# Joined VectorE products and a permuted fine-factor read in an S4 convolution on one Trainium2 core

## The chip, the core and the metric

The kernel runs on one core of a Trainium2 chip. Five engines work side by side there, each with its own instruction stream: TensorE (PE in the profile, with its weight loads as PEld), VectorE (DVE), ScalarE (ACT), GpSimd (POOL) and SyncE (SP). The last two serve here mostly to issue DMAs. The metric is the time of one execution in microseconds of device time; the median of three runs of the kernel before is 1786.69 us (1786.42 to 1787.71).

## The reference

The block has two halves: a state-space convolution over the sequence and then a gated MLP, each behind a layer norm modulated by a conditioning vector `c`. Cut to what matters:

```python
mod = (silu(c) @ w_mod)                    # sa, ca, ga, sb, cb, gb
h = layernorm(x) * (1 + ca) + sa
x = x + ga * S4(h)                         # the part that the change touches
h = layernorm(x) * (1 + cb) + sb
x = x + gb * gMLP(h)                       # w_in, gelu, spatial mix w_sp, w_out

def S4(u):                                 # L = 2048 steps, D = 576 channels, N = 128 states
    P = exp(dt * A * l)                    # complex, (D, N, L)
    K = einsum("dn,dnl,dn->dl", C, P, dt * B).real
    y = irfft(rfft(pad(u)) * rfft(pad(K)))[:L] + u * Dskip
```

The kernel does not build P. It writes each position l as a coarse and a fine part. The complex power is then a product of a coarse factor (32 values per state) and a fine factor (64 values), and K is a sum over the 128 states of such products, which is a matrix product. The convolution runs through a two-stage Fourier transform done with matrix products.

## The kernel before

**The convolution stage** is the function `ssm`. Its work comes in 36 groups of 16 channels (`NG = 36`), and a loop over ticks (40 of them) starts one step of several groups in each tick, so that steps of different groups overlap. For a group g, one step per tick after the other:

- `t_unit` makes phases of the coarse and fine factors with four small TensorE products (L455), rounds them away on ScalarE and VectorE (L456, L457), and takes an absolute value on VectorE (L459). The tile name is `ft`; the phase `f` and its absolute value `ct` are two tiles out of 5 buffers.
- `s_unit`, one tick later, turns `ct` and `f` into cosines and sines on ScalarE (L464, L465), 1024 elements each: half of them are for fine factors, half for coarse ones.
- `e_unit` (L443 to L447) makes the magnitudes `et` for three groups at once every third tick: 1024 fine and 512 coarse values.
- `p_unit`, two ticks after `t_unit`, multiplies magnitudes with cosines and sines in five VectorE instructions (L475 to L479). `pg` holds the coarse real part (512) and the fine real part (1024); the imaginary parts overwrite `et`.
- `kg_unit` forms K: 16 channels, each a product of coarse factors (weights, 128 x 32) with fine factors (moving, 128 x 64), real and imaginary part added up in PSUM. That is 32 products (L489). The profile shows two MATMUL records for each float32 product, so 64 records. Four channels go to four 32-row strips of PSUM, and so to four column strips of TensorE. ScalarE then copies the 256 columns of K into `kab` with a permutation, written with a step of four elements (L492).
- `d_unit` adds the skip term to one column (L496) and `k1_unit` starts the Fourier transform of K with 8 products (L506), whose result ScalarE or VectorE copies into `k1` (L513, L511).

Beside that, the input's spectrum runs chunk by chunk (five channel chunks of 128, 128, 128, 128 and 64; 36 pieces of 512 columns in all):

- `u_unit` transforms a piece (L548), copies it to `ue` (L549), and two DMAs on GpSimd's queue (L551, L552) write `us`, the same piece with its two partition halves swapped.
- `z_unit` makes the filter's spectrum in PSUM (L561) and multiplies it on VectorE with `ue` into `za` (L562) and with `us` into `zb` (L563).
- `v_unit`, a tick later, transforms back with two products added in one PSUM bank, one from `za` (L570) and one from `zb` (L571). ScalarE copies the result (L572) and GpSimd's queue stores it (L573).
- `y_unit` reads what was stored back and finishes the transform (L615, L617).

**What sets the order.** Within a tick the source calls `y_load`, `u_load`, `z_unit`, `p_unit`, `t_unit`, `s_unit`, `v_unit`, `kg_unit`, `u_unit`, `k1_unit`, `y_unit`, `d_unit`, `e_unit`. A scheduler then orders each engine's instructions by its own model; only what goes through `tied` is kept in the written order. In most ticks TensorE's order is: Z (L561, 4 products), V (L570, L571), K's 32 products (L489), U (L548), K1 (L506). Every third tick has the six magnitude products (L443, L446) as well, and phase products (L455) follow in between.

**Tail.** After the ticks the last two chunks are finished in a hand-written, pinned order, mixed with the first steps of the MLP (`mlp.start...`). Tiles of the spectrum's pools (`ue`, `us`, `za`, `zb`) are used again there for stores, reloads and residual inputs. After that comes the MLP (all its rows show the helper line L145).

Of the kernel before, what the change touches and what calls it, by code (L numbers as in the profile page):

```python
# [31 lines left out]
def consts():  # L32
    a = np.arange(32)
    k1 = np.arange(32)
    k2 = np.arange(64)
    beta = np.arange(64)
    b = np.where(beta < 32, 32 + beta, 63 - beta)
    b4 = b.reshape(4, 16).T.reshape(64)
    ang = 2 * np.pi * np.outer(a, k1 + 0.25) / 32
    r1 = np.zeros((2, 128, 128))  # L40
    for j in range(4):
        s = slice(32 * j, 32 * j + 32)
        r1[0, s, s] = np.cos(ang)
        r1[1, s, s] = -np.sin(ang)
    r1t = np.zeros((128, 16, 2, 32))
    st4 = np.zeros((128, 16, 2, 64))
    for t in range(16):
        for g in range(4):
            th = ang + 2 * np.pi * b4[4 * t + g] * (k1 + 0.25) / 2048
            s = slice(32 * g, 32 * g + 32)  # L50
            r1t[s, t, 0] = np.cos(th)
            r1t[s, t, 1] = -np.sin(th)
            hh, g2 = divmod(g, 2)
            o = slice(32 * g2, 32 * g2 + 32)
            st4[64 * g2:64 * g2 + 32, t, hh, o] = np.cos(th).T / 2048
            st4[64 * g2 + 32:64 * g2 + 64, t, hh, o] = -np.sin(th).T / 2048

    import ml_dtypes
    part = np.stack([r1t[32 * g:32 * g + 32].sum(0) for g in range(4)])
    cs = np.zeros((128, 16, 2, 32))  # L60
    for i in range(3):
        rows = part.astype(ml_dtypes.bfloat16).astype(np.float64)
        for r in ((0, 3, 5), (1, 4), (2,))[i]:
            cs[r::32] = rows
        part = part - rows
    msk = np.zeros((128, 2))
    for g in range(0, 128, 32):
        msk[g + 3:g + 6, 0] = -1.0
        msk[g + 5, 1] = -1.0

    def forward(th):
        tr, ti = np.cos(th), np.sin(th)
        return np.block([[tr, ti], [-ti, tr]])

    st2 = np.stack([forward(-2 * np.pi * np.outer(b4, k + 0.25 + 32 * k2) / 2048) for k in range(32)], 1)
    th = -2 * np.pi * np.outer(b4, k2) / 64
    tr, ti = np.cos(th).T, np.sin(th).T
    st3a, st3b = np.zeros((128, 128)), np.zeros((128, 128))
    for h, sg in ((0, 1.0), (1, -1.0)):
        rows = slice(64 * h, 64 * h + 64)  # L80
        st3a[rows, 0::2] = sg * tr
        st3a[rows, 1::2] = -sg * ti
        st3b[rows, 0::2] = ti
        st3b[rows, 1::2] = tr
    eye = np.eye(8)
    rgt = np.zeros((6, 8, 8, 32))
    rge = np.zeros((6, 8, 8, 32))
    rpe = np.zeros((6, 8, 8, 64))
    rgt[:3] = eye[None, :, :, None] * a
    rgt[3:] = eye[None, :, :, None]  # L90
    rge[:3] = eye[None, :, :, None] * (64 * a)
    rge[3:] = eye[None, :, :, None]
    rpe[:3] = eye[None, :, :, None] * b
    rpt = np.zeros((6, 8, 8, 32))
    rpt[:3] = eye[None, :, :, None] * (np.arange(32) + 0.5)
    half = np.concatenate([rgt.reshape(48, 256), rpe.reshape(48, 512), rpt.reshape(48, 256)], axis=1)
    sel = np.zeros((112, 1536))
    sel[:48, :1024] = sel[64:, :1024] = half
    sel[:48, 1024:1280] = sel[64:, 1280:] = rge.reshape(48, 256)
    ones = np.zeros((128, 128))  # L100
    ones[::32] = 1.0
    f = np.float32
    fwd = forward(th).reshape(2, 16, 4, 128).transpose(2, 1, 0, 3).reshape(128, 128)
    small = np.concatenate([np.eye(128), r1[0], r1[1], fwd, st3a, st3b, ones], axis=1)
    return {"c_small": small.astype(f), "c_st": st2.astype(f), "c_r1t": r1t.astype(f), "c_st4": st4.astype(f),
            "c_sel": sel.astype(ml_dtypes.bfloat16), "c_cs": cs.astype(ml_dtypes.bfloat16), "c_msk": msk.astype(f)}
# [51 lines left out]
def ssm(tc, I, x1_d, consts_s, dram, mod_d, mlp):  # L158
# [5 lines left out]
    with ExitStack() as ctx:  # L164
# [217 lines left out]
        def ln_stats(i):  # L382
# [2 lines left out]
            r = ep.tile([128, 4], F32, name="r")  # L385
            if i < 2:
                junk = ep.tile([128, 4, HC], F32, name="st1o").rearrange("p (a b) d -> p a (b d)", a=2)
                ss = ep.tile([128, 4], F32, name="ss")
                for b in range(4):
                    A.activation(junk[:, 0], x[:, b], AF.Copy, accum_out=nm[:, b:b + 1])  # L390
                V.tensor_scalar(nm, nm, -1.0 / D, None, op0=ALU.mult)
# [56 lines left out]

        def t_unit(g):
            c, gi = divmod(g, 9)  # L450
            f = tb.tile([128, 2, 512], F32, name="ft", bufs=5)
            pa = ps2()
            for k, (n, c0) in enumerate((("lc", 768), ("la", 0))):
                for h, (l, r) in enumerate(zip(halves(lt[n, c], gi), rows(c0, 256))):
                    T.matmul(pa[:, h].rearrange("p (c k j) -> p k c j", c=8, k=2)[:, k], l, r, start=True, stop=True)  # L455
            A.activation(f, pa, AF.Identity, bias=magic)  # L456
            V.scalar_tensor_tensor(f, f, MAGIC, pa, op0=ALU.subtract, op1=ALU.subtract)  # L457
            ct = tb.tile([128, 2, 512], F32, name="ft", bufs=5)
            V.tensor_single_scalar(ct.bitcast(I32), f.bitcast(I32), 0x7FFFFFFF, op=ALU.bitwise_and)  # L459
            tt[g] = (f, ct)  # L460

        def s_unit(g):
            f, ct = tt[g]
            A.activation(ct, ct, AF.Sin, bias=halfpi, scale=-TWO_PI)  # L464
            A.activation(f, f, AF.Sin, scale=-TWO_PI)  # L465

        def p_unit(g):

            f, ct = tt[g]
            e = et.pop(g)  # L470
            p = tb.tile([128, 1536], F32, name="pg")
            pr, pi = [t[:, :1024].rearrange("p (c s j) -> p c s j", c=16, s=2) for t in (p, e)]
            gr, gi = [t[:, 1024:].rearrange("p (c a) -> p c a", c=16) for t in (p, e)]
            c3, s3 = [x.rearrange("p h (c k j) -> p k (h c) j", c=8, k=2) for x in (ct, f)]
            V.tensor_tensor(gr, gi, c3[:, 1], op=ALU.mult)  # L475
            V.tensor_tensor(pr, pi, c3[:, 0, :, None, :].to_broadcast([128, 16, 2, 32]), op=ALU.mult)
            V.tensor_tensor(gi, gi, s3[:, 1], op=ALU.mult)
            V.scalar_tensor_tensor(pi[:, :, 0], s3[:, 0], -1.0, pi[:, :, 0], op0=ALU.mult, op1=ALU.mult)
            V.tensor_tensor(pi[:, :, 1], s3[:, 0], pi[:, :, 1], op=ALU.mult)  # L479
            tt[g] = (pr, pi, gr, gi)  # L480

        def kg_unit(g):
            pr, pi, gr, gi = tt.pop(g)
            pm = ps1()
            for i in range(4):
                for x_, y_, st in ((gr, pr, True), (gi, pi, False)):
                    for j in range(4):
                        c = 4 * i + j
                        T.matmul(pm[32 * j:32 * j + 32, 64 * i:64 * i + 64], x_[:, c], y_[:, c].rearrange("p s j -> p (s j)"),  # L489
                                 start=st, stop=not st, skip_group_check=True)  # L490
            kk = kab[g] = tb.tile([128, 4, 64], F32, name="kab")
            A.activation(kk.rearrange("p i (b w) -> p i w b", w=4), pm[:, :256].rearrange("p (i w b) -> p i w b", i=4, w=4), AF.Copy)  # L492

        def d_unit(g):
            kk = kab[g]
# [34 lines left out]
        def part(n, bufs=2):  # L530
            return sb.tile([128, 512], F32, name=n, bufs=bufs)

        def by(t, c):
            return t.rearrange("p (k d) -> p k d", d=CHW[c])

# [7 lines left out]

        def u_unit(c, i):
            u1 = st.pop((c, i))
            ue = part("ue", 4)
            pm = ps1()
            T.matmul(pm, fwd, u1, start=True, stop=True)  # L548
            A.activation(ue, pm, AF.Copy)  # L549
            us = part("us", 4)  # L550
            G.dma_start(us[:64], ue[64:])  # L551
            G.dma_start(us[64:], ue[:64])  # L552
            st[c, i] = (ue, us)

        def z_unit(c, i):
            ue, us = st.pop((c, i))
            w = CHW[c]
            za, zb = part("za"), part("zb")
            pm = ps1()
            for j, k in enumerate(range(32)[kr(c, i)]):  # L560
                T.matmul(pm[:, w * j:w * j + w], cst[k // 8][:, k % 8], k1t[c][:, k, :w], start=True, stop=True)  # L561
            V.tensor_tensor(za, pm, ue, op=ALU.mult)  # L562
            V.tensor_tensor(zb, pm, us, op=ALU.mult)  # L563
            st[c, i] = (za, zb)

        def v_unit(c, i):
            za, zb = st.pop((c, i))
            v = part("ue", 4) if c == NC - 1 and i > 1 else part("v")
            pm = ps1()
            T.matmul(pm, inva, za, start=True, stop=False)  # L570
            T.matmul(pm, invb, zb, start=False, stop=True)  # L571
            A.activation(v, pm, AF.Copy)  # L572
            G.dma_start(v_d[c][:, kr(c, i)], by(v, c))  # L573

        def y_vload(c, q):
# [1 line left out]
            w = CHW[c]  # L577
            rows = v_d[c].rearrange("(b h g) k d -> b h (g k) d", b=16, h=2)[bs].rearrange("b h p d -> p h b d")
            if c == NC - 1:
                t = part("ue", 4)  # L580
                st["yv", c, q] = t[:, :4 * w], t[:, 4 * w:]
                for hh in range(2):
                    S.dma_start(by(t[:, 4 * w * hh:4 * w * hh + 4 * w], c), rows[:, hh])
                return
            if c == NC - 2 and q < 2:
                vt = [part("za"), part("zb")]
            else:
                vt = [part("u1", 5)[:, :4 * w] for _ in range(2)]
            st["yv", c, q] = vt
# [3 lines left out]
        def y_xload(c, q):  # L593
# [3 lines left out]
            elif c == NC - 1:  # L597
                xb = mlp.x1l[:, 4 * q - 4:4 * q]
            else:
                xb = by(part("us", 4) if c == NC - 2 or (c, q) == (2, 3) else part("xb"), c)  # L600
                S.dma_start(xb, I["x"][:, bs, chan(c)])
            st["y", c, q] = xb, bs

# [1564 lines left out]
```

## Time and profile before

| what | value |
|---|---|
| median of 3 runs | 1786.69 us (1786.42 to 1787.71) |
| the profiled execution: time, span | 1784.31 us, 1782.5 us |
| mean granted TensorE clock | 0.964 |
| TensorE busy over the span | 1664.0 us, 93% |
| VectorE busy over the span | 1265.7 us, 71% |
| ScalarE busy over the span | 854.0 us, 48% |
| first and last start of K's products (L489) | 72.2 us, 396.4 us |

The profiled execution took 2.4 us less than the median of the runs. The page cuts the span in 40 slices of 44.6 us; a digit is the busy share of an engine in tenths. The convolution stage fills about the first nine slices. A row of a group names line, engine, operation, tiles and shapes, how often it ran, the busy time and the mean length of one, and then the idle time of the engine just before it with what ended that time. In an answer in order of time, a row has start, length, engine, line, operation, and how many instructions were merged. The length of a VectorE or ScalarE instruction is longer than the distance to the next start, because neighbours overlap a little; what one instruction costs its engine is read from start to start.

### The profile page before, as it was taken

To read this page: it belongs to the slowest core of one execution; us is meant where nothing else is said; L and a number is where in the kernel's file an instruction comes from. 1 tells how busy PE (TensorE), PEld (TensorE's weight loads), DVE (VectorE), ACT (ScalarE), POOL (GpSimd) and SP (SyncE) were. 2 spreads that over 40 slices of the span, in tenths; PEclk is the share of its full clock that TensorE was granted. 3 is DMA by queue.
4 is the path that set the end of the run, shared out by engine and by line. 5 is a ranking of instruction groups with operands and counts; after the bars stand their busy time and mean duration, and the time that the engine had idled before them with its cause. 6 is when DMAs were issued, how large, how long until landed. Compare 5 with 4: busy or idle time off the path is not lost.

```text
span 1782.5 us, 36327 instructions
## 1 busy us (share of the span) xinstructions
PE 1664.0 (93%) x15094; PEld 1239.3 (70%) x15094; DVE 1265.7 (71%) x2331; ACT 854.0 (48%) x1130; POOL 247.4 (14%) x400
## 2 busy tenths in 40 slices
PE   4487899997899999999989999999999999999999
PEld 1243455565455545777877888888888888888887
DVE  6864999966999998788899777688344478344432
ACT  5877999854477666455434444234232223122210
POOL 4311232333122211000000000000111100111100
PEclk8586999998999999999999999999999999999999
DMA  9356645579689779777665886773766572556531
GB/s 276 117 175 202 175 124 167 167 210 301 210 251 293 243 227 268 279 250 254 234 215 163 285 301 236 268 247 121 251 222 231 196 233 99 192 195 218 192 111 40
DMA packets 183380, 376.04 MB, mean 211 GB/s; under 512 B 39360, under 2 KB 103488, under 8 KB 182448
## 3 DMA queue, kind: packets, MB, share of 16 engines
q1 hardware_dynamic: 140416, 175.05, 32.2%
q0 software_dynamic: 36896, 172.01, 28.7%
q10 hardware_dynamic: 5904, 26.67, 3.7%
q8 instruction: 118, 1.93, 0.4%
q14 instruction: 46, 0.38, 0.1%
HBM read 262.93 MB, written 101.31 MB: 204 GB/s over the span
## 4 chain that ended last, share of the span: by engine, by line
PE 57%; DVE 14%; DMA 5%; issue 3%; ACT 1%; POOL 0%; SPq 0%; ACTq 0%; DVEq 0%; POOLq 0%
PE ps L145 54%; DVE bsz L145 2%; DMA zset<-set_d 2%; DMA wsst<-in_w_spT 1%; DVE zset L145 1%; DVE gt L145 1%; DVE n L145 1%; DVE rq L145 1%; DVE wsp L145 1%; PE pk L145 1%; DVE wso L145 1%; DVE raw L145 1%; DVE nt L145 1%; DMA z_d<-z 1%; PE pk L561 1%
## 5 line engine op out<-in xcount | busy, mean ns | idle before, releaser
L145 PEld LDWEIGHTS <-zset 128*128 128x128 f16 x7182 | 701.9, 98 | 93.9 <-DVE zset L145 8.8
L145 PE MATMUL ps<-wsp,zset 128*128 128x256 f16 x6048 | 667.7, 273 | 8.4 <-DVE zset L145 6.8
L145 PE MATMUL pz<-wz,nt 128*128 128x512 f16 (+1 forms) x1120 | 222.3, 358 | 10.6 <-DVE nt L145 4.5
L145 ACT ACTIVATE z<-gt 128x1024 f16<-128x1024 f32 x56 | 59.0, 1054 | 281.7 <-DVE gt L145 281.7
L145 PEld LDWEIGHTS <-nt 128*128 128x128 f16 x1120 | 108.8, 98 | 117.9 <-DVE nt L145 5.9
L145 DVE SCALAR_TENSOR_TENSOR gt<-ps,sc,bsp 128x512 f32<-128x512 f32 x36 | 27.0, 749 | 204.8 <-PE ps L145 203.0
L1876 POOL DMA_DIRECT2D zset<-set_d x96 | 51.0, 532 | 870.5 <-PE ps L145 623.2
L145 PE MATMUL ps<-wout,z 128*128 128x288 f16 x1344 | 170.0, 286 | 0.0
L145 PEld LDWEIGHTS <-z 128*128 128x128 f16 x1344 | 131.5, 98 | 33.0
L145 PE MATMUL ps<-n2o,zset 128*128 128x256 f16 x1134 | 128.2, 273 | 0.0
L145 DVE SCALAR_TENSOR_TENSOR gt<-ps,sc,gt 128x512 f32<-128x512 f32 (+1 forms) x180 | 122.2, 696 | 7.9 <-DVE gt L145 0.5
L145 DVE TENSOR_TENSOR raw<-raw 128x512 f32<-128x512 f32 (+2 forms) x228 | 119.1, 528 | 10.6 <-DMA raw<-z_d 6.3
L145 ACT ACTIVATE zset<-raw 128x1792 f16<-128x1792 f32 x48 | 81.2, 1691 | 63.2 <-PE ps L145 39.5
L145 DVE TENSOR_TENSOR zset<-raw,zset 128x1792 f16<-128x1792 f32 x48 | 97.0, 2020 | 17.4 <-ACT zset L145 16.2
L145 DVE TENSOR_TENSOR z<-ps,z 128x512 f32<-128x512 f32 (+1 forms) x126 | 72.0, 598 | 36.8 <-ACT z L145 25.1
L145 ACT ACTIVATE wsp<-raw,sc 128x1792 f16<-128x1792 f32 x25 | 44.6, 1785 | 42.9 <-DVE raw L145 35.2
L145 ACT ACTIVATE z<-z,sc 128x1024 f32<-128x1024 f32 x21 | 24.1, 1148 | 75.6 <-DVE z L145 71.9
L457 DVE SCALAR_TENSOR_TENSOR ft<-ft,ps 128x1024 f32<-128x1024 f32 x36 | 43.7, 1214 | 22.4 <-ACT ft L456 22.4
L145 ACT ACTIVATE z<-z,nm,r 128x1152 f32<-128x1152 f32 x24 | 31.4, 1342 | 51.1 <-DVE nm L145 30.5
L145 ACT ACTIVATE z<-pz,sc 128x512 f32<-128x512 f32 (+1 forms) x96 | 51.5, 584 | 8.8 <-DMA z_d<-z 4.8
L145 PE MATMUL ps<-n2q,wf 128*128 128x512 f16 x252 | 55.7, 379 | 0.0
L506 PEld LDWEIGHTS pk<-small,kab 128*64 128x64 f32 x576 | 34.2, 145 | 28.9 <-issue 17.3
(359 smaller groups left out, 2507.6 us busy)
## 6 DMA issues: line engine op xcount, KB each, us to landing
zset<-set_d POOLq DMA_DIRECT2D x96, 896.0 KB, 4.9
raw<-z_d SPq DMA_DIRECT2D x48, 512.0 KB, 5.5
set_d<-zset ACTq DMA_DIRECT2D x24, 896.0 KB, 6.0
z_d<-z POOLq DMA_DIRECT2D x32, 576.0 KB, 9.0
zset<-wa_d POOLq DMA_DIRECT2D x18, 896.0 KB, 4.9
raw<-in_w_spT SPq DMA_DIRECT2D x25, 512.0 KB, 4.8
set_d<-zset SPq DMA_DIRECT2D x12, 896.0 KB, 5.9
u_d<-st1o POOLq DMA_DIRECT2D x16, 576.0 KB, 4.0
```

Source lines behind the costliest of these rows:

```text
L145: return self.tc.keep_in_program_order(f(*a, **k))
L457: V.scalar_tensor_tensor(f, f, MAGIC, pa, op0=ALU.subtract, op1=ALU.subtract)
L506: T.matmul(pm[64 * ri:64 * ri + 64, 128 * i:128 * i + 128], kk[:, i], r1[ri], start=True, stop=True, skip_group_check=True)
L561: T.matmul(pm[:, w * j:w * j + w], cst[k // 8][:, k % 8], k1t[c][:, k, :w], start=True, stop=True)
L1876: self.nc.gpsimd.dma_start(o, self.set_d[f, j - 1] if j else self.wa_d[f])
```

## The change

Four edits go together. All of them are in the convolution stage.

- **Coarse factors.** Cosine and sine of a group now lie in one tile of 2 x 1024 (`cs`, 3 buffers). `p_unit` makes the real and the imaginary coarse factor with one VectorE instruction of 1024 elements, in which the magnitude is read twice (a step of zero). Both land in `pg`, which grows from 1536 to 2048 columns. Four instructions stand where five stood.
- **Spectrum products.** `ue` and `us` become the two halves of one tile `uu`, `za` and `zb` of one tile `zz`. `z_unit` has one VectorE instruction of 1024 elements that reads the PSUM bank twice. Buffer counts stay (4 and 2 pairs).
- **K's layout.** The moving operand of K's products is read permuted: the 64 fine factors of a channel are taken with a step of 16 elements (64 bytes) between one and the next, four at a time, instead of one behind the other. K then stands in PSUM in the order in which `kab` wants it, and ScalarE's copy is straight.
- **Tail.** Where the tail took single `ue` and `us` tiles, it now takes halves of `uu` tiles (`half`), two uses per tile. One small statistics tile (`ss`) has one buffer.

How many instructions there are on TensorE, ScalarE, GpSimd and SyncE stays as it was, and so does TensorE's order of steps in the ticks; VectorE has 72 fewer, and the scheduler places some of its products differently within a tick.

```diff
         def t_unit(g):
-            f = tb.tile([128, 2, 512], F32, name="ft", bufs=5)
+            cs = tb.tile([128, 2, 2, 512], F32, name="ft", bufs=3)
+            ct, f = cs[:, 0], cs[:, 1]
...
         def p_unit(g):
...
-            p = tb.tile([128, 1536], F32, name="pg")
+            p = tb.tile([128, 2048], F32, name="pg")
             pr, pi = [t[:, :1024].rearrange("p (c s j) -> p c s j", c=16, s=2) for t in (p, e)]
-            V.tensor_tensor(gr, gi, c3[:, 1], op=ALU.mult)
-            V.tensor_tensor(pr, pi, c3[:, 0, :, None, :].to_broadcast([128, 16, 2, 32]), op=ALU.mult)
-            V.tensor_tensor(gi, gi, s3[:, 1], op=ALU.mult)
-            V.scalar_tensor_tensor(pi[:, :, 0], s3[:, 0], -1.0, pi[:, :, 0], op0=ALU.mult, op1=ALU.mult)
-            V.tensor_tensor(pi[:, :, 1], s3[:, 0], pi[:, :, 1], op=ALU.mult)
+            gri = p[:, 1024:].rearrange("p (x c a) -> p x c a", x=2, c=16)
+            c3, s3 = cs[:, 0, 0], cs[:, 0, 1]
+            V.tensor_tensor(gri, e[:, None, 1024:].rearrange("p x (c a) -> p x c a", c=16).to_broadcast([128, 2, 16, 32]), cs[:, 1], op=ALU.mult)
+            V.tensor_tensor(pr, pi, c3[:, :, None, :].to_broadcast([128, 16, 2, 32]), op=ALU.mult)
+            V.scalar_tensor_tensor(pi[:, :, 0], s3, -1.0, pi[:, :, 0], op0=ALU.mult, op1=ALU.mult)
+            V.tensor_tensor(pi[:, :, 1], s3, pi[:, :, 1], op=ALU.mult)
...
         def kg_unit(g):
-                        T.matmul(pm[32 * j:32 * j + 32, 64 * i:64 * i + 64], x_[:, c], y_[:, c].rearrange("p s j -> p (s j)"),
+                        T.matmul(pm[32 * j:32 * j + 32, 64 * i:64 * i + 64], x_[:, c], y_[:, c].rearrange("p s (h t) -> p t (s h)", h=2),
                                  start=st, stop=not st, skip_group_check=True)
-            A.activation(kk.rearrange("p i (b w) -> p i w b", w=4), pm[:, :256].rearrange("p (i w b) -> p i w b", i=4, w=4), AF.Copy)
+            A.activation(kk, pm[:, :256].rearrange("p (i b) -> p i b", i=4), AF.Copy)
...
+        spare = []
+
+        def half():
+            if not spare:
+                uu = sb.tile([128, 2, 512], F32, name="uu", bufs=4)
+                spare.extend((uu[:, 1], uu[:, 0]))
+            return spare.pop()
...
         def u_unit(c, i):
-            ue = part("ue", 4)
+            uu = sb.tile([128, 2, 512], F32, name="uu", bufs=4)
-            A.activation(ue, pm, AF.Copy)
-            us = part("us", 4)
-            G.dma_start(us[:64], ue[64:])
-            G.dma_start(us[64:], ue[:64])
+            A.activation(uu[:, 0], pm, AF.Copy)
+            G.dma_start(uu[:64, 1], uu[64:, 0])
+            G.dma_start(uu[64:, 1], uu[:64, 0])
...
         def z_unit(c, i):
-            za, zb = part("za"), part("zb")
+            zz = sb.tile([128, 2, 512], F32, name="zz")
-            V.tensor_tensor(za, pm, ue, op=ALU.mult)
-            V.tensor_tensor(zb, pm, us, op=ALU.mult)
+            V.tensor_tensor(zz, pm[:, None, :].to_broadcast([128, 2, 512]), uu, op=ALU.mult)
...
         def v_unit(c, i):
-            v = part("ue", 4) if c == NC - 1 and i > 1 else part("v")
+            v = half() if c == NC - 1 and i > 1 else part("v")
-            T.matmul(pm, inva, za, start=True, stop=False)
-            T.matmul(pm, invb, zb, start=False, stop=True)
+            T.matmul(pm, inva, zz[:, 0], start=True, stop=False)
+            T.matmul(pm, invb, zz[:, 1], start=False, stop=True)
```

More of the change, by code (lines that the diff above doesn't have):

```diff
@@ L98, in consts @@
     sel[:48, :1024] = sel[64:, :1024] = half
-    sel[:48, 1024:1280] = sel[64:, 1280:] = rge.reshape(48, 256)
+    sel[:48, 1024:1280] = sel[64:, 1280:1536] = rge.reshape(48, 256)
     ones = np.zeros((128, 128))
@@ L387, in ln_stats @@
                 junk = ep.tile([128, 4, HC], F32, name="st1o").rearrange("p (a b) d -> p a (b d)", a=2)
-                ss = ep.tile([128, 4], F32, name="ss")
+                ss = ep.tile([128, 4], F32, name="ss", bufs=1)
                 for b in range(4):
@@ L457, in t_unit @@
             V.scalar_tensor_tensor(f, f, MAGIC, pa, op0=ALU.subtract, op1=ALU.subtract)
-            ct = tb.tile([128, 2, 512], F32, name="ft", bufs=5)
             V.tensor_single_scalar(ct.bitcast(I32), f.bitcast(I32), 0x7FFFFFFF, op=ALU.bitwise_and)
-            tt[g] = (f, ct)
+            tt[g] = cs
         def s_unit(g):
-            f, ct = tt[g]
+            ct, f = tt[g][:, 0], tt[g][:, 1]
             A.activation(ct, ct, AF.Sin, bias=halfpi, scale=-TWO_PI)
@@ L467, in p_unit @@
         def p_unit(g):
-            f, ct = tt[g]
+            cs = tt[g].rearrange("p x h (c k j) -> p k x (h c) j", c=8, k=2)
             e = et.pop(g)
-            p = tb.tile([128, 1536], F32, name="pg")
+            p = tb.tile([128, 2048], F32, name="pg")
             pr, pi = [t[:, :1024].rearrange("p (c s j) -> p c s j", c=16, s=2) for t in (p, e)]
[L473 to L477, printed above, removed]
-            V.scalar_tensor_tensor(pi[:, :, 0], s3[:, 0], -1.0, pi[:, :, 0], op0=ALU.mult, op1=ALU.mult)
-            V.tensor_tensor(pi[:, :, 1], s3[:, 0], pi[:, :, 1], op=ALU.mult)
-            tt[g] = (pr, pi, gr, gi)
+            gri = p[:, 1024:].rearrange("p (x c a) -> p x c a", x=2, c=16)
[4 more added lines that the diff above has]
+            V.tensor_tensor(pi[:, :, 1], s3, pi[:, :, 1], op=ALU.mult)
+            tt[g] = (pr, pi, gri[:, 0], gri[:, 1])
         def kg_unit(g):
@@ L545, in u_unit @@
             u1 = st.pop((c, i))
-            ue = part("ue", 4)
+            uu = sb.tile([128, 2, 512], F32, name="uu", bufs=4)
             pm = ps1()
             T.matmul(pm, fwd, u1, start=True, stop=True)
-            A.activation(ue, pm, AF.Copy)
-            us = part("us", 4)
-            G.dma_start(us[:64], ue[64:])
-            G.dma_start(us[64:], ue[:64])
-            st[c, i] = (ue, us)
+            A.activation(uu[:, 0], pm, AF.Copy)
+            G.dma_start(uu[:64, 1], uu[64:, 0])
+            G.dma_start(uu[64:, 1], uu[:64, 0])
+            st[c, i] = uu
         def z_unit(c, i):
-            ue, us = st.pop((c, i))
+            uu = st.pop((c, i))
             w = CHW[c]
-            za, zb = part("za"), part("zb")
+            zz = sb.tile([128, 2, 512], F32, name="zz")
             pm = ps1()
@@ L561, in z_unit @@
                 T.matmul(pm[:, w * j:w * j + w], cst[k // 8][:, k % 8], k1t[c][:, k, :w], start=True, stop=True)
-            V.tensor_tensor(za, pm, ue, op=ALU.mult)
-            V.tensor_tensor(zb, pm, us, op=ALU.mult)
-            st[c, i] = (za, zb)
+            V.tensor_tensor(zz, pm[:, None, :].to_broadcast([128, 2, 512]), uu, op=ALU.mult)
+            st[c, i] = zz
         def v_unit(c, i):
-            za, zb = st.pop((c, i))
-            v = part("ue", 4) if c == NC - 1 and i > 1 else part("v")
+            zz = st.pop((c, i))
+            v = half() if c == NC - 1 and i > 1 else part("v")
             pm = ps1()
-            T.matmul(pm, inva, za, start=True, stop=False)
-            T.matmul(pm, invb, zb, start=False, stop=True)
+            T.matmul(pm, inva, zz[:, 0], start=True, stop=False)
+            T.matmul(pm, invb, zz[:, 1], start=False, stop=True)
             A.activation(v, pm, AF.Copy)
@@ L579, in y_vload @@
             if c == NC - 1:
-                t = part("ue", 4)
+                t = half()
                 st["yv", c, q] = t[:, :4 * w], t[:, 4 * w:]
@@ L585, in y_vload @@
             if c == NC - 2 and q < 2:
-                vt = [part("za"), part("zb")]
+                zz = sb.tile([128, 2, 512], F32, name="zz")
+                vt = [zz[:, 0], zz[:, 1]]
             else:
@@ L599, in y_xload @@
             else:
-                xb = by(part("us", 4) if c == NC - 2 or (c, q) == (2, 3) else part("xb"), c)
+                xb = by(half() if c == NC - 2 or (c, q) == (2, 3) else part("xb"), c)
                 S.dma_start(xb, I["x"][:, bs, chan(c)])
```

## The prediction

> **What bounds the kernel now.** I read the page's header and slices first, then busy times by stage, then TensorE's waits in the stage that changes.
>
> ```profile
> span 1782.5 us, 36327 instructions
> ...
> PE   4487899997899999999989999999999999999999
> ...
> DVE  6864999966999998788899777688344478344432
> ACT  5877999854477666455434444234232223122210
> ...
> PEclk8586999998999999999999999999999999999999
> ```
>
> All of the change lies in the convolution stage, about the first nine slices. From the fourth slice to the eighth TensorE, VectorE and ScalarE all stand at 7 to 9 tenths, so the page can't say which of them is worth time. In busy times by stage (stretch, its length, then busy time and instructions of TensorE, its weight loads, VectorE, ScalarE, GpSimd, granted clock, DMA share, GB/s):
>
> ```profile
> 72.00:176.00 104.00, 79.87 (x1073) 41.75 (x1073) 66.64 (x147) 76.31 (x100) 26.39 (x40) 0.68 0.60 186
> 176.00:409.60 233.60, 216.83 (x3036) 131.46 (x3035) 199.89 (x301) 196.92 (x256) 74.15 (x125) 0.98 0.63 174
> 250.85:272.95 22.10, 20.74 (x304) 12.10 (x304) 21.92 (x32) 21.85 (x30) 9.15 (x16) 1.00 0.57 162
> 409.60:1782.50 1372.90, 1338.90 (x10804) 1055.51 (x10802) 946.22 (x1738) 531.52 (x684) 125.38 (x199) 0.99 0.66 220
> ```
>
> The second row is the stage proper (28 of the 36 groups), the third is three of its ticks. Busy times of VectorE and ScalarE count overlapping ends and look fuller than they are. TensorE has 233.60 - 216.83 = 16.8 us free in 233.6 us. What it waits for there:
>
> ```profile
> PE pk L561 <- ACT v L572: 5.8, 6, 1.5
> PE ps L443 <- ACT et L444: 2.8, 4, 0.9
> PE ps L443 <- DVE ft L457: 2.8, 2, 2.3
> PE pk L506 <- ACT ue L549: 1.8, 1, 1.8
> PE pk L561 <- DVE k L511: 1.1, 2, 0.7
> ```
>
> So TensorE is the bound, with short waits for ScalarE (10.4 us in these rows) and VectorE (3.9 us), mostly for a PSUM bank to be emptied. A faster VectorE or ScalarE can win part of these waits and no more; any time added to TensorE's own products is paid nearly whole. Behind 409.6 us is the MLP, bound by TensorE and untouched: it moves by what the stage gains or loses.
>
> **Part 1, VectorE's joined products.** In order of time:
>
> ```profile
> 260.43 0.68 DVE L475 TENSOR_TENSOR pg<-et,ft 128x512 f32<-128x512 f32 x1
> 261.03 1.21 DVE L476 TENSOR_TENSOR pg<-et,ft 128x1024 f32<-128x1024 f32 x1
> 262.17 0.68 DVE L562 TENSOR_TENSOR za<-pk,ue 128x512 f32<-128x512 f32 x1
> 262.77 0.67 DVE L563 TENSOR_TENSOR zb<-pk,us 128x512 f32<-128x512 f32 x1
> 263.37 0.68 DVE L477 TENSOR_TENSOR et<-et,ft 128x512 f32<-128x512 f32 x1
> ```
>
> From start to start, 512 elements cost 0.60 us (260.43 to 261.03, 262.17 to 262.77) and 1024 cost 1.14 us (261.03 to 262.17). A joined pair saves 2 x 0.60 - 1.14 = 0.06 us. There are two joins per group and 36 of each: 72 x 0.06 = 4.3 us of VectorE. The source read twice has a row close by: the L476 instruction already reads its cosine twice, and costs the same per element. In return consumers start later. V's first product (L570) used to wait for `za` alone and now waits for the pair, 0.54 us longer; and the whole pair now waits for the swap DMAs:
>
> ```profile
> L562 DVE TENSOR_TENSOR za<-pk,ue 128x512 f32<-128x512 f32 x32 | 21.9, 684 | 6.5 <-PE pk L570 5.1 <-PE pk L561 1.0
> L563 DVE TENSOR_TENSOR zb<-pk,us 128x512 f32<-128x512 f32 x32 | 21.8, 681 | 2.0 <-DMA us<-ue 1.3 <-PE pk L571 0.7
> ```
>
> VectorE waited only 1.3 us in all for those DMAs, and V runs a tick behind Z, so I cost both at nothing; if that cover were gone, 1.3 us and 36 x 0.54 = 19 us are the ceilings. The 4.3 us are no gain by themselves: they can only shorten TensorE's 3.9 us of waits for VectorE.
>
> **Part 2, ScalarE's straight copy of K.** Groups of the stage, then ScalarE in order of time:
>
> ```profile
> L444 ACT ACTIVATE et<-ps 128x1024 f32<-128x1024 f32 x24 | 24.9, 1039 | 0.4 <-PE ps L443 0.3
> L492 ACT ACTIVATE kab<-pk 128x256 f32<-128x256 f32 x28 | 18.1, 648 | 4.2 <-PE pk L489 4.2
> L572 ACT ACTIVATE v<-pk 128x512 f32<-128x512 f32 x30 | 18.0, 600 | 19.2 <-PE pk L571 15.6 <-issue 2.4 <-ACT ft L465 1.2
> ```
>
> ```profile
> 246.22 0.58 ACT L572 ACTIVATE v<-pk 128x512 f32<-128x512 f32 x1
> 246.70 0.63 ACT L492 ACTIVATE kab<-pk 128x256 f32<-128x256 f32 x1
> 247.10 0.65 ACT L549 ACTIVATE ue<-pk 128x512 f32<-128x512 f32 x1
> 247.64 1.12 ACT L456 ACTIVATE ft<-ps,consts_s 128x1024 f32<-128x1024 f32 x1
> ```
>
> The straight copies give (1039 - 600) / 512 = 0.86 ns per element and 600 - 439 = 161 ns fixed. The permuted copy, written with a step of 16 bytes, streams at (648 - 161) / 256 = 1.90 ns, 2.2 times as long. A straight 256 would take 161 + 220 = 381 ns, 0.27 us less until `kab` is ready. From start to start the copy costs 0.40 us; straight 512 cost 0.48 and 0.54, so straight 256 would cost 0.26 to 0.32. I take 0.11 us a group, 36 x 0.11 = 4.0 us of ScalarE, which can shorten only the 10.4 us of waits.
>
> **Part 3, the permuted read on TensorE.** The 64 columns of each of K's products are now fetched one by one from places 64 bytes apart. In order of time:
>
> ```profile
> 262.80 0.32 PE L489 MATMUL pk<-pg 128*32 128x64 f32 x8
> 262.94 0.29 PE L489 MATMUL pk<-et 128*32 128x64 f32 x8
> 263.05 0.29 PE L489 MATMUL pk<-pg 128*32 128x64 f32 x8
> ...
> 263.61 0.29 PE L489 MATMUL pk<-et 128*32 128x64 f32 x8
> 263.83 1.13 PE L548 MATMUL pk<-u,small 128*128 128x512 f32 x2
> ```
>
> Eight bundles of eight records (four channels side by side) follow each other every 0.11 us, and K takes 263.83 - 262.80 = 1.03 us of TensorE per group. No matmul of this kernel streams its moving operand with a step, so this cost is bounded by neighbours. Lower end: nothing; the permuted read is as fast. [...] Nearest is the copy of K, the only SBUF access here whose neighbouring 4-byte elements lie 16 bytes or more apart, at 2.2 times. I take twice: 8 x 0.11 = 0.9 us more per group.
>
> [...]
>
> **The sum**, against the profiled execution (1784.31 us, 2.4 us below the median):
> - K on TensorE in the stage proper: 28 x 0.9 = +25.2 us.
> - Absorbed: of the 16.8 us that TensorE is free there I take half, -8.4 us. ScalarE and VectorE each get lighter by 0.1 us per group while the tick grows, so their late releases shrink; the dense ends of the third ticks remain. The savings of parts 1 and 2 are spent here.
> - The first eight groups (72 to 176 us): TensorE is free for 24 us, so of 8 x 0.9 = 7.2 us I let 1.5 us through, against 1.5 us that two lighter engines win there.
> - Memory moves and the tail: the halves of one tile now pair two uses. The tail's chain is ruled by the store and reload below, which the change keeps, so 0, with 2 us either way.
>
> ```profile
> 429.91 6.07 DMA v_d<-ue
> 436.03 2.85 DMA ue<-v_d
> ```
>
> Sum 25.2 - 8.4 = +16.8, less about 1.8 us for the savings that still show where TensorE isn't the bound: +15 us. 1784.3 + 15 = 1799.3 for such an execution, 1786.7 + 15 = 1801.7 for the median. This case's own range: all free time absorbed, +8.4 us, 1795; none absorbed and streaming 2.2 times as long, 28 x 1.06 + 3 = +33 us, 1820.
>
> **The rivals.**
> - *Faster: the permuted read costs nothing.* Decided by K's bundles staying 0.11 us apart. Then the lighter engines shorten TensorE's waits: a third of 10.4 + 3.9, 4.8 us, less what later starts cost: -4.5 us, 1782. For it: PSUM reads of ScalarE with a wide step cost nothing (the copy of `k`, 599 ns for 512, below); against it the row of `kab`. Chance 0.28.
> - *No gain: the read is free, and TensorE stays the bound,* with V's later start taking back what ScalarE's waits give: 1786.7. Chance 0.12.
> - [...] Chance 0.13.
>
> ```profile
> L513 ACT ACTIVATE k<-pk 128x512 f32<-128x512 f32 x23 | 13.8, 599 | 5.4 <-PE pk L506 5.3
> ```
>
> The rival that the change doesn't do what it says is small: its VectorE instructions are fewer by 72 in any case.
>
> **How the numbers follow.** The doubled read has 0.47. Within 0.2% (3.6 us), about what a measurement of this kernel can tell from no change, lie most of the second rival and a part of the first. Faster: 0.24 of the first, 0.02 of the second, 0.26. Same: 0.04, 0.08 and 0.01 of the doubled read, 0.13. Slower: 0.46, 0.13 and 0.02, 0.61. The range leaves out the far slower rival (0.13) and the quicker end of the first (0.07): 1781, a little under its 1782, to 1830, past 1820 for the part of streaming costs between two and four times.
>
> **What the profile after would show.** K's bundles of eight 0.22 us apart instead of 0.11, and 64 records in about 1.9 us; the copy of K at about 380 ns; the joined products at about 1214 ns, 72 of them; TensorE's free time in the stage down to about 8 us; the stage longer by 15 us and the MLP as long as before. It is wrong if the bundles stay at 0.11 us, or if V (L570) begins to wait for the joined product.

## The result, and the profile after

| | before | after |
|---|---|---|
| median | 1786.56 us (4 runs, 1782.38 to 1787.71) | 1801.49 us (4 runs, 1798.72 to 1803.26) |
| ratio, 95% interval | | 1.0086 (1.0065 to 1.0108) |
| profiled execution: time, span | 1784.31 us, 1782.5 us | 1798.72 us, 1796.9 us |
| K's products per group on TensorE | 1.03 us | 1.97 us |
| ScalarE's copy of K | 648 ns | 381 ns |
| VectorE instructions | 2331 | 2259 |

The kernel became 14.9 us slower, 0.86%. The header, the slices and the granted clock on the page of the changed kernel:

```profile
span 1796.9 us, 36230 instructions
...
PE   4486999998799989999989999999999999999999
...
DVE  6975888865898998788899777689344468344432
ACT  4887988854377666445434343334222124122210
...
PEclk8597999999899999999999999999999999999999
```

TensorE now stands at 9 from the fifth slice to the ninth, where its fifth had 8. VectorE lost a tenth in slices 5 to 8, and ScalarE in 6 and 7: two engines were relieved and the third was loaded. Busy time by stage, with the bounds moved to the same places in the work (the columns are those of the prediction):

```profile
170.00:419.49 249.49, 239.41 (x3027) 152.42 (x3019) 196.45 (x242) 192.03 (x256) 71.55 (x125) 0.99 0.58 162
419.49:1796.90 1377.41, 1341.19 (x10802) 1056.55 (x10802) 945.49 (x1734) 531.81 (x684) 125.61 (x199) 0.99 0.66 219
```

The stage proper grew from 233.60 to 249.49 us, by 15.9. TensorE's busy time in it grew by 239.41 - 216.83 = 22.6 us, and its free time fell from 16.8 to 10.1 us. The main reason stands in the products of K, in order of time:

```profile
262.11 0.41 PE L488 MATMUL pk<-pg 128*32 128x64 f32 x8
262.33 0.44 PE L488 MATMUL pk<-et,pg 128*32 128x64 f32 x8
262.57 0.43 PE L488 MATMUL pk<-pg 128*32 128x64 f32 x8
...
263.70 0.45 PE L488 MATMUL pk<-et,pg 128*32 128x64 f32 x8
264.08 0.70 PE L555 MATMUL pk<-u,small 128*128 128x512 f32 x1
```

The bundles of eight records follow each other every 0.23 us where they stood 0.11 us apart, and a group's products take 264.08 - 262.11 = 1.97 us. On the other side of the account, ScalarE's copy and VectorE's joined products came out as their rows had promised (groups of the stage):

```profile
L491 ACT ACTIVATE kab<-pk 128x256 f32<-128x256 f32 x28 | 10.7, 381 | 16.5 <-PE pk L488 16.4
```

```profile
L568 DVE TENSOR_TENSOR zz<-pk,uu 128x1024 f32<-128x1024 f32 x32 | 39.1, 1222 | 17.2 <-PE pk L576 7.2 <-PE pk L567 5.5 <-DMA uu<-uu 4.5
L475 DVE TENSOR_TENSOR pg<-et,ft 128x1024 f32<-128x1024 f32 x27 | 33.0, 1221 | 6.4 <-PE pk L488 6.3
```

Both engines now sit idle more often until TensorE is done (16.4 us before the copies, 7.2 + 5.5 us before the joined spectrum products, 6.3 us before the coarse factors). TensorE's own waits shrank in return; ScalarE's release of a PSUM bank to Z cost 5.8 us before:

```profile
PE ps L443 <- ACT et L444: 2.2, 4, 0.6
PE ps L443 <- DVE ft L458: 2.2, 1, 2.2
PE pk L567 <- ACT v L577: 1.5, 3, 0.7
PE pk L505 <- ACT uu L556: 1.1, 1, 1.1
```

Where the 14.4 us between the two profiled executions came from is best read at three marks of the same work: K1 of one group early in the stage (here is its row in each kernel), the last K1, and the MLP's first product with `n2q` (a tile that the MLP multiplies with its weights).

```profile
190.28 1.09 PE L506 MATMUL pk<-small,kab 128*64 128x128 f32 x16
```

```profile
184.59 1.09 PE L505 MATMUL pk<-small,kab 128*64 128x128 f32 x16
```

| mark, us | before | after | before, second profile |
|---|---|---|---|
| K1 early in the stage | 190.28 | 184.59 | 189.59 |
| last K1 | 407.64 | 417.50 | 406.77 |
| first product with `n2q` | 693.4 | 706.5 | 695.0 |
| span | 1782.5 | 1796.9 | 1785.2 |

Against the first profile of before, the changed kernel is 5.7 us ahead when the stage gets going, loses 15.6 us to the last K1 (232.9 us instead of 217.4), and then 3.2 and 1.3 us more. The last two need not be work of the change: the second profile of the unchanged kernel has 2.4 and 1.1 us of them as well.

### The profile page after: what moved, and what is told of

The parts are those of the page before. It is cut to its first block, busy times and chain, and to the rows that moved or that the text cites. A ratio compares the mean times of both kernels' runs of the same rounds, so it can differ in the third digit from the quotient of the medians.

```text
span 1796.9 us, 36230 instructions
## 1 busy us (share of the span) xinstructions
PE 1683.2 (94%) x15094; PEld 1260.5 (70%) x15094; DVE 1261.7 (70%) x2259; ACT 848.1 (47%) x1130; POOL 245.4 (14%) x400
## 3 DMA queue, kind: packets, MB, share of 16 engines
q8 instruction: 118, 1.93, 0.4%
## 4 chain that ended last, share of the span: by engine, by line
PE 58%; DVE 13%; issue 7%; DMA 5%; ACT 1%; POOL 0%; SPq 0%; ACTq 0%; DVEq 0%; POOLq 0%
PE ps L145 50%; DMA zset<-set_d 2%; DVE bsz L145 2%; PE pk L488 2%; DVE n L145 1%; PE pk L555 1%; DVE zset L145 1%; PE pk L575 1%; DVE rq L145 1%; PE pk L567 1%; PE pk L576 1%; DVE wso L145 1%; DVE gt L145 1%; PE pk L505 1%; DMA wst<-in_w_in 1%
## 5 line engine op out<-in xcount | busy, mean ns | idle before, releaser
L488 PE MATMUL pk<-et,pg 128*32 128x64 f32 x1152 | 66.9, 293 | 0.9 <-DVE et L478 0.9
L488 PE MATMUL pk<-pg 128*32 128x64 f32 x1152 | 65.8, 293 | 0.1
L458 DVE SCALAR_TENSOR_TENSOR ft<-ft,ps 128x1024 f32<-128x1024 f32 x36 | 43.8, 1217 | 22.6 <-ACT ft L457 22.6
```

## The experiments

My theory was that the permuted read on TensorE is the whole loss, and that the joins and the straight copy are worth little. The rival was that the joined products cost the time, since their consumers start later. Each version was timed beside new runs of the kernel before, so the median of before differs from set to set (1785.93 to 1787.4 us).

### The read and the straight copy alone

```diff
 (the kernel before)
-  y_[:, c].rearrange("p s j -> p (s j)")
+  y_[:, c].rearrange("p s (h t) -> p t (s h)", h=2)
-  A.activation(kk.rearrange("p i (b w) -> p i w b", w=4), pm[:, :256].rearrange("p (i w b) -> p i w b", i=4, w=4), AF.Copy)
+  A.activation(kk, pm[:, :256].rearrange("p (i b) -> p i b", i=4), AF.Copy)
```

> The kernel before with the permuted read of the fine factors and the straight copy of K, and without the joined products. Theory (the permuted read costs TensorE about 0.9 us per group and is the whole loss): eight records every 0.23 us instead of 0.11, the stage longer by 14 to 24 us, a little more than the whole change costs, since VectorE isn't relieved; ratio 1.008 to 1.013. Rival (the joined products cause the loss, because consumers start later): within 2 us of before, ratio 0.999 to 1.001.

Measured: 1803.1 us against 1787.4 us, ratio 1.0085 (1.0071 to 1.0100): 15.7 us slower, the whole loss without a single join. K's records, straight ones in the kernel before (first fence) and permuted ones here (second), over all groups:

```profile
L489 PE MATMUL pk<-pg 128*32 128x64 f32 x1152 | 42.4, 234 | 1.3 <-DVE pg L476 1.3
```

```profile
L489 PE MATMUL pk<-pg 128*32 128x64 f32 x1152 | 66.4, 293 | 1.4 <-DVE pg L476 1.4
```

### The joined products alone

```diff
 (the changed kernel)
-  y_[:, c].rearrange("p s (h t) -> p t (s h)", h=2)
+  y_[:, c].rearrange("p s j -> p (s j)")
-  A.activation(kk, pm[:, :256].rearrange("p (i b) -> p i b", i=4), AF.Copy)
+  A.activation(kk.rearrange("p i (b w) -> p i w b", w=4), pm[:, :256].rearrange("p (i w b) -> p i w b", i=4, w=4), AF.Copy)
```

> The whole change without the permuted read and without the straight copy: joined products, joined tiles and the tail's halves alone. Theory: VectorE has 72 instructions and about 4 us less, which shortens TensorE's waits for it a little: 0 to 4 us faster, ratio 0.998 to 1.000. Rival (joined products cause the loss): 8 to 15 us slower, ratio 1.004 to 1.008.

Measured: 1787.32 us against 1787.4 us, ratio 0.9997 (0.9981 to 1.0012). The rival falls: the joins don't cost the time. Alone they win nothing that these runs can tell from zero either. One row shows where part of VectorE's 4 us may have gone:

```profile
L568 DVE TENSOR_TENSOR zz<-pk,uu 128x1024 f32<-128x1024 f32 x32 | 39.1, 1221 | 13.6 <-DMA uu<-uu 8.4 <-PE pk L576 4.1 <-PE pk L567 0.7
```

VectorE now waits 8.4 us for the DMAs that swap the halves; when the product with `us` was an instruction of its own, it waited 1.3 us. A second profile of this version has 5.5 us there.

### The straight copy alone

The copy can be straight without a permuted read. The order of K's 64 positions comes from a constant of the next stage but one (`c_st`, whose rows are summed over by Z); its rows can be permuted on the host, with no instruction more on the chip.

```diff
 (the kernel before)
-  st2 = np.stack([forward(-2 * np.pi * np.outer(b4, k + 0.25 + 32 * k2) / 2048) for k in range(32)], 1)
+  st2 = np.stack([forward(-2 * np.pi * np.outer(b, k + 0.25 + 32 * k2) / 2048) for k in range(32)], 1)
-  A.activation(kk.rearrange("p i (b w) -> p i w b", w=4), pm[:, :256].rearrange("p (i w b) -> p i w b", i=4, w=4), AF.Copy)
+  A.activation(kk, pm[:, :256].rearrange("p (i b) -> p i b", i=4), AF.Copy)
```

> The kernel before with the straight copy of K alone (the order made good by the constant), straight read, no joined products. Theory: 36 copies shorter by 0.27 us, ScalarE relieved by about 4 us; what reaches the end is a part of TensorE's waits for ScalarE: 1 to 4 us faster, ratio 0.998 to 0.9995. Rival (the copy's end sits on the path between K's products and the next step in every group): 0.27 x 28 = 7.6 us faster, ratio 0.996.

Measured: 1786.97 us against 1787.4 us, ratio 0.9997 (0.9983 to 1.0010). The copies took 390 ns each, 36 x 0.26 = 9.3 us less of ScalarE's rows, and none of it can be told from zero at the end. Expected were 1 to 4 us.

### Joins and straight copy, without the permuted read

```diff
 (the changed kernel)
-  np.outer(b4, k + 0.25 + 32 * k2)
+  np.outer(b, k + 0.25 + 32 * k2)
-  y_[:, c].rearrange("p s (h t) -> p t (s h)", h=2)
+  y_[:, c].rearrange("p s j -> p (s j)")
```

> The whole change with TensorE's old straight read; K's new order is made good by a permuted constant of the filter's Fourier stage, so that ScalarE's copy stays straight at no cost. Theory: records of K stay 0.11 us apart for eight, the copy takes 0.38 us, the time is that of the forecast's faster rival: 3 to 8 us faster than before, ratio 0.9955 to 0.998. Rival (joined products cause the loss): slower than before by 5 to 15 us.

Measured: 1782.84 us against 1787.4 us, ratio 0.9976 (0.9960 to 0.9993). This version beats both kernels: 4.6 us under the one before, and 18.7 us under the changed one (timed in another set), from which only the way to K's order differs. So the permuted read by itself costs about 18.7 us, and the rest of the change wins about 4.6 us.

### Which steps of a read cost, and whether four strips hold each other up

```diff
 (the kernel before; w: elements from one fetch to the next)
+  def step(y, w): return y.rearrange("p (a w) -> p w a", w=w)
-  K:  y_[:, c] straight
+  K:  by group: straight, w=2, w=4, w=8, w=16, adjacent pairs 16 apart
-  T.matmul(pm, fwd, u1, ...)
+  T.matmul(pm, fwd, (u1, step(u1, 2), step(u1, 4), step(u1, 16))[i % 4], ...)
-  zip(halves(lb, gi), rows(256, 512))
+  zip(halves(lb, gi), [(x, step(x, 8), step(x, 32))[g % 3] for x in rows(256, 512)])
```

> The kernel before with the moving operand of three products read with other steps (elements are taken in another order, so what is computed is not the reference's): K's products by group, in turn straight, with steps of 2, 4, 8 and 16 float32 elements, and in adjacent pairs 16 elements apart; U's products (512 columns, whole array) by piece, straight, step 2, 4 and 16; the magnitudes' bf16 products (512 columns) by group, straight, step 8 and step 32. [...]

The run is a single execution of 1816.8 us. The first bundle of K's products of six groups in a row, each followed by the U product that came next (start, length; K of a group takes from its row to U's row):

```profile
265.00 0.32 PE L500 MATMUL pk<-pg 128*32 128x64 f32 x8
266.03 1.96 PE L559 MATMUL pk<-u,small 128*128 128x512 f32 x2
...
275.20 0.32 PE L500 MATMUL pk<-pg 128*32 128x64 f32 x8
276.27 1.12 PE L559 MATMUL pk<-u,small 128*128 128x512 f32 x2
...
283.22 0.42 PE L500 MATMUL pk<-pg 128*32 128x64 f32 x8
285.22 1.17 PE L559 MATMUL pk<-u,small 128*128 128x512 f32 x2
...
291.03 0.43 PE L500 MATMUL pk<-pg 128*32 128x64 f32 x8
293.05 2.04 PE L559 MATMUL pk<-u,small 128*128 128x512 f32 x2
...
302.34 0.42 PE L500 MATMUL pk<-pg 128*32 128x64 f32 x8
304.30 1.96 PE L559 MATMUL pk<-u,small 128*128 128x512 f32 x2
...
311.91 0.32 PE L500 MATMUL pk<-pg 128*32 128x64 f32 x8
312.96 1.13 PE L559 MATMUL pk<-u,small 128*128 128x512 f32 x2
```

| read of the moving operand | K per group, us | U per piece, us of busy time |
|---|---|---|
| straight | 1.03 | 1.12 |
| step 2 (8 bytes) | 1.07 | 1.17 |
| adjacent pairs, 64 bytes apart | 1.05 | |
| step 4 (16 bytes) | 2.00 | 2.04 |
| step 8 (32 bytes) | 2.02 | |
| step 16 (64 bytes) | 1.96 | 1.96 |

Here the cost sets in between a step of 8 bytes (1.07 us) and one of 16 (2.00 us), and the two larger steps tried cost no more (2.02 and 1.96 us). Read in pairs of neighbours, at the one distance tried, 64 bytes, K took 1.05 us. U, one product of 128 x 128 at a time, goes from 1.12 to 1.96 us much as K's four strips go from 1.03 to 1.96, so nothing here shows the four strips holding each other up, and the far slower rival, to which the prediction gave 0.13, falls. The bf16 products say more:

```profile
296.05 0.39 PE L443 MATMUL ps<-sel,lb 48*128 48x512 bf16 x2
296.38 0.39 PE L446 MATMUL pk<-sel,lb 112*128 112x512 bf16 x1
296.70 1.06 PE L443 MATMUL ps<-sel,lb 48*128 48x512 bf16 x2
297.69 0.60 PE L446 MATMUL pk<-sel,lb 112*128 112x512 bf16 x2
```

Straight, a pair of them side by side takes 296.38 - 296.05 = 0.33 us; with a step of 16 bytes 297.69 - 296.70 = 0.99 us, three times as long. So it isn't a doubling everywhere: 0.99 us over 512 columns is 1.93 ns a column, and U's 1.96 us over two records of 512 columns is 1.9 ns too. In these products a column read with a step of 16 bytes or more took about 1.9 ns, and how many times as long that is depends on the straight read: 0.64 ns a column in the bf16 pair (0.33 us over 512), 1.1 ns in U (1.12 us over 1024).

### The joins one at a time, and the start of the stage

```diff
 (joins and straight copy, straight read; spectrum product apart)
-  V.tensor_tensor(zz, pm[:, None, :].to_broadcast([128, 2, 512]), uu, op=ALU.mult)
+  V.tensor_tensor(zz[:, 0], pm, uu[:, 0], op=ALU.mult)
+  V.tensor_tensor(zz[:, 1], pm, uu[:, 1], op=ALU.mult)
 (or instead: coarse factors apart)
-  V.tensor_tensor(gri, e[:, None, 1024:]...to_broadcast([128, 2, 16, 32]), cs[:, 1], op=ALU.mult)
+  for x in range(2):
+      V.tensor_tensor(gri[:, x], e[:, 1024:]..., cs[:, 1, x], op=ALU.mult)
```

> The version with joined products, straight read and straight copy, but the spectrum product again as two instructions of 512 elements on the joined tiles. Theory (a joined spectrum product saves 0.06 us of VectorE and has to wait for the swapped half): equal to the joined one within 2 us, ratio to before 0.996 to 0.999. Rival (the joined spectrum product is what wins the 4.6 us): back to the time before, ratio 0.9995 to 1.001.

> The version with joined products, straight read and straight copy, but the coarse factors again as two instructions of 512 elements. Together with the version whose spectrum product is apart it says which join goes with the straight copy to make the 4 us lead at the start of the stage (K1 at 186.3 instead of 190 us). If the coarse join does: K1 at 189 to 192 us and a ratio to before of 0.9985 to 1.0005. If neither join alone is needed: K1 at 186 to 187 us and a ratio of 0.997 to 0.9985.

Second profiles of four kernels without any edit, to see what differs between executions:

> The kernel before, unchanged, for a second profile: how far the start of the stage (K's first Fourier products, K1, at 180.7 us in the first profile) and the way from the last K1 product (407.6 us) to the MLP's first product with n2q (693.4 us, 285.8 us later) differ between executions of one kernel. If the six microseconds that the changed kernel was ahead at 174 us are the change's, this profile is at 180.7 again within 1 us; if they are a matter of the granted clock in the first 180 us, it may be anywhere from 174 to 182.

> The version with joined products, straight read and straight copy once more, for the same question: its K1 stood at 177.0 us where before had 180.7. Same reading: 177 within 1 us if it is the kernel's, 174 to 182 if it is the clock's.

> The joined products alone for a second profile: K1 stood at 191.05 us. Within 1 us again if the start of the stage is a property of the kernel; 186 to 193 if it is not.

> The straight copy alone for a second profile: K1 stood at 192.57 us. Within 1 us again if the start of the stage is a property of the kernel; 186 to 193 if it is not.

| kernel | coarse join | spectrum join | straight copy | early K1, us | ratio to before |
|---|---|---|---|---|---|
| before | no | no | no | 190.28, again 189.59 | 1 |
| copy alone | no | no | yes | 192.57, again 192.45 | 0.9997 |
| coarse apart | no | yes | yes | 193.24 | 0.9994 (0.9983 to 1.0004) |
| joins alone | yes | yes | no | 191.05, again 188.26 | 0.9997 |
| spectrum apart | yes | no | yes | 186.24 | 0.9985 (0.9973 to 0.9998) |
| joins and copy | yes | yes | yes | 186.63, again 186.31 | 0.9976 (0.9960 to 0.9993) |

Four rows of early K1 carry the reading below. They belong, in turn, to the joins and copy, to the spectrum apart, to the coarse factors apart, and to the permuted read and the copy without a join (the first experiment):

```profile
186.63 1.09 PE L505 MATMUL pk<-small,kab 128*64 128x128 f32 x16
186.24 1.09 PE L505 MATMUL pk<-small,kab 128*64 128x128 f32 x16
193.24 1.09 PE L506 MATMUL pk<-small,kab 128*64 128x128 f32 x16
190.10 1.09 PE L506 MATMUL pk<-small,kab 128*64 128x128 f32 x16
```

With the spectrum product apart the median was 1783.19 us (before: 1785.93 us), with the coarse factors apart 1784.85 us (before: 1786.01 us). These runs point to the coarse join, together with the straight copy, as what brings the lead of 3 to 4 us at the start of the stage, and with it most of the gain; the spectrum join adds nothing that they can tell from zero. But this is not shown. The intervals of the two versions overlap. The one profile with the coarse factors apart was taken on another chip than the other two versions' and in an execution of 1791.66 us, 6.8 us over that version's median, and its early K1 lies above the 189 to 192 us expected. The first experiment speaks for the joins too: with the same permuted read and the same copy its early K1 stood at 190.10 us without the joins, and at 184.59 us with them in the changed kernel. In the medians that lead doesn't show: the ratios to before are 1.0085 without the joins and 1.0086 with them.

Three of the four second profiles repeat the early K1 of the table within 1 us; the joins alone moved by 2.8 us, so there the expectation of 1 us fell. The expectations for the kernel before and for the joins with the copy name the K1 one group earlier (180.7 and 177.0 us): the second profiles have it at 180.02 and 175.89 us, the latter 1.1 us off.

Why the first 190 us gain isn't settled. In them TensorE runs at a lower granted clock than behind them (0.99 from 190 to 420 us in the kernel before). From 72 to 190 us it was 0.69 and 0.72 in the two profiles of the kernel before, 0.75 in both of the joins with the copy, and 0.83 in the changed kernel. But a higher clock doesn't explain the lead by itself: the read and copy without a join had 0.78, more than the joins with the copy, and its early K1 stood at 190.10 us, no earlier than before. None of these runs set the clock by itself.

## Why the prediction was right

The time, 1801.49 us against 1801.7 us predicted, came out through the step that was forecast: the permuted read costs TensorE about twice the time (1.97 us per group against 1.03), and in this stage TensorE has little room for it (16.8 us free of 233.6). That it came out within 0.2 us is luck, because errors of 2 to 3 us cancelled. By the version with the joins and the copy alone, the read costs 18.7 us where the forecast had 25.2 - 8.4 = 16.8, and the rest of the change wins 4.6 us where the forecast took 1.8 off.

- **The permuted read** (taken at +0.9 us per group, by twice the streaming time): 0.94 us. The choice of twice went by the row of ScalarE's copy, and that row has a cost of the same size in it: 1.90 ns per element written with a step of 16 bytes, against about 1.9 ns per column here. That the two have one cause is not shown. "Twice" is about right for the float32 products alone (1.96 us against 1.03 for K, 1.96 against 1.12 for U); the bf16 pair took three times as long.
- **The range past 1820** (streaming between two and four times as long, and the 0.13 of the far slower rival): no run shows four times. The slowest step tried took K from 1.03 to 2.02 us per group; the bf16 pair, which the forecast doesn't price, went from 0.33 to 0.99 us.
- **Absorbed** (8.4 of 16.8 us): 6.7 us, from 16.8 to 10.1. The stage proper grew by 15.9 us, forecast 16.8 before the small gains. The parts don't fully explain it: 28 groups at 0.94 us are 26.3 us, but TensorE's busy time grew by only 22.6. The other products took 3.7 us less, for which the sum has no term; without that the stage would have grown by 19.6 us. About half of it lies in the products of Z and in V's first product, whose rows in the two stretches went from 37.0 to 36.1 and from 32.5 to 31.5 us; the rest is not settled.
- **The first groups** (1.5 us let through, 1.5 us won): this term was mis-sized. The changed kernel is 5.0 to 5.7 us ahead there. I had priced the two lighter engines by their saved microseconds; the runs show 3 to 4 us of the lead in the joins with the copy as well, which have no permuted read.
- **Tail and MLP** (0, with 2 us either way): +4.5 us against the first profile, +1.0 us against the second. That profile of before was a quick one behind the stage, which hid the term above in the comparison of the two profiles.
- **Parts 1 and 2** (the savings spent as absorption): alone they gave ratios of 0.9997 each, as costed. That V begins later cost nothing that can be seen: no row of TensorE's waits in the stage names the joined product. The swap DMAs, which I let go at 1.3 us, became a wait of 4.5 us before the joined product in the changed kernel, but VectorE had that time.
- **The faster rival** (1782 us if the read cost nothing) had the right size: with the read taken out and the order made by a constant, the kernel takes 1782.84 us. But it had the wrong way there: it took the time out of TensorE's waits in the stage. In the two profiles of that version 3 to 4 us are won before the early K1, and from there to the last K1 only 0.3 to 1.5 us.
- **A slip in reading the slices**: the three engines stand at 7 to 9 tenths from the fifth slice on, not the fourth, where VectorE has 4. No term of the sum rests on it.

## What to carry to other kernels

Before a permutation is moved from one engine to another, see which engine the stage waits for: here 0.27 us of latency per group on an engine with room were bought with 0.94 us on the one without. A permutation can sometimes be pushed further, into a constant that is summed over, where here it cost nothing that the runs can tell (1786.97 us against 1787.4). And read a strided access by its bytes: with a step of 8 bytes, or with pairs of neighbours, K's products stayed within 4% of their straight time (1.07 and 1.05 us against 1.03), and with steps of 16, 32 and 64 bytes they took 1.96 to 2.02 us, about 1.9 ns a column.

## What the runs showed that I had not expected

- In these runs the cost of a read with a step of 16 bytes or more is a time and not a factor: about 1.9 ns a column for TensorE's moving reads in float32 and bf16 and, in the profile of before, 1.90 ns an element for ScalarE's writes with a step of 16 bytes. For bf16 products that is three times the straight read (0.99 against 0.33 us).
- Four column strips of TensorE pay it side by side: K's products, four strips at once, went to 1.96 us from 1.03, and a whole-array product to 1.96 from 1.12 us of busy time.
- A join that saves VectorE 0.06 us per group in a stage bound by TensorE showed no gain by itself; together with a shorter copy the kernel was 3 to 4 us ahead before that stage. The profiles point to the coarse join for it, and the cause stays open.
